# Putting the conditional slots without tokens in front of those that have tokens, in an attention and mixture-of-experts kernel

## The chip, the cores and the metric

The kernel runs on one core of a Trainium2 chip. The metric is the device time of one execution in microseconds (us). Timed executions of the kernel before took 885.78 us in the median of three (880.81 to 892.82). The profile is that of another, separate execution, which took 846.87 us and has a span of 845.1 us from its first instruction to its last, so a step read in the profile is a little shorter than in the timed runs. Engines are called PE (TensorE, matrix multiplication), PEld (its weight loads), DVE (VectorE), ACT (ScalarE), POOL (GpSimd) and SP (SyncE, which issues most transfers here). A "q" after a name (SPq, PEldq, POOLq) means the sequencer of that engine: branches, semaphores, register loads and the issuing of transfers.

## What is computed

Two blocks, one after the other. The first is windowed attention (8 batches, 8 heads, 576 positions, head size 64). Its output becomes a table of 4608 tokens of width 512. The second is a mixture of experts without dropped tokens: each token goes to the one expert with the highest logit, and that expert is a two-layer network.

```python
logits = x @ w_gate                       # x: 4608 x 512, 8 experts
expert_idx = np.argmax(logits, axis=1)
...                                       # gate_w: softmax probability of that expert
for e in range(E):
    h = np.maximum(x_sorted[lo:hi] @ w1[e], 0.0)    # 512 -> 1024
    y_sorted[lo:hi] = h @ w2[e]                     # 1024 -> 512
return gate_w[:, None] * y
```

How many tokens an expert gets is known only on the chip. The kernel therefore works in slots of 128 tokens of one expert. 4608 tokens make 36 full slots, and since each of the 8 experts may end with a partly filled slot, there can be up to 43. Slots 0 to 35 are always worked on. Slots 36 to 42 are conditional: each stands inside a runtime `If`, which lets it run only if it has tokens. With these inputs 39 slots have tokens, so 36, 37 and 38 run and 39 to 42 are skipped.

## The kernel before

Each slot needs three transfers: `x`, 128 rows of tokens (257 KB); `w1`, the first weight matrix of its expert (2 MB); `w2`, the second (2 MB). Two buffers hold `w1` and two hold `w2`; even slots use one of each, odd slots the other. If a slot has the same expert as the slot two before it, its weights are already there, and the transfer is issued with a condition that is false, so that it moves nothing. Three buffers hold `x`.

```python
NSLOT = (N + E * 127) // 128      # 43
SURE = N // 128                   # 36
...
"eidx": np.tile(np.minimum(np.arange(E1), E - 1), (128, 1)),   # "no expert" is read as expert 7
...
# new[j]: does slot j need other weights than slot j - 2?
nc.vector.tensor_tensor(out=new[:, lo - j0 : K], in0=exs[:, lo:j1],
                        in1=exs[:, lo - 2 : j1 - 2], op=OP.not_equal)
...
def fetch_x(j):                                                            # line 676
    x = xs[j] = mpool.tile([128, ROW], F32, tag="x", name=f"x_{j}", bufs=3)
    at0 = nc.sync.value_load(basei[:, n : n + 1], ...)                     # line 679
    read_bucket(nc.sync.dma_start(x, bucket[ds(at0, 128), :]), b)          # line 680

def fetch_w(j, dst, src):
    rv = nc.sync.value_load(exi[:, n : n + 1], ...)                        # line 684
    if j >= 2:
        kw["cond"] = nc.sync.value_load(newi[:, n : n + 1], ...) > 0       # line 687
    nc.sync.dma_start(dst[j % 2], src[ds(rv, 1)]..., **kw)                 # line 688

wanted = []
for j in range(NSLOT):
    wanted += [(j, "x", 0, j - 1), (j, "w1", 0, j - 1), (j, "w2", 1, j - 1)]
done = [0, 0]          # slots whose first / second layer has been written into the program

def fetch():           # issues, in the order of the list, all that may be issued by now
    while wanted and wanted[0][0] in where and done[wanted[0][2]] >= wanted[0][3]:
        ...

def across(j):         # turns x of slot j: 4 PE transposes and a DVE copy (lines 713, 715)
    ...

for j in range(NSLOT):
    if j >= SURE:
        while late:
            late.pop(0)()                          # the scatter of the slot before
        guards.close()
        guards.enter_context(tc.If(live[0] > j))   # line 725
    ...
    for fg in range(2):                            # first layer
        ...                                        # 32 matmuls into ph (line 739), twice
        if fg == 0:
            ...
            if j + 1 in xs:
                nxt = across(j + 1)
        else:
            done[0] = j + 1
            fetch()
    ...                                            # second layer: 16 matmuls into py (line 763)
    nc.scalar.activation(y, py, AF.Copy, scale=x[:, DM : DM + 1])          # line 767
    late.append(scatter)                           # indirect DMA on POOL (line 772)
    done[1] = j + 1
    fetch()
    xt = nxt
while late:
    late.pop(0)()
guards.close()                                     # line 790
```

So the transfers of a slot are issued while the slot before it is being worked on, and for conditional slots the issue stands inside the `If` of that slot before.

Of the kernel before, what the change touches and what calls it, by code (L numbers as in the profile page):

```python
# [10 lines left out]
F32 = mybir.dt.float32  # L11
I32 = mybir.dt.int32
AF = mybir.ActivationFunctionType
OP = mybir.AluOpType
# [6 lines left out]
N, DM, E, F = B * S, H * DH, 8, 1024  # L21
# [9 lines left out]
NSLOT = (N + E * 127) // 128  # L31
NROWS = E * CAP + 128
NOWHERE = 1.0e6
E1 = E + 1
SURE = N // 128


READY = [max(0, -(-(S * (b + 1) - E * 127) // 128)) for b in range(B)]
READY[B - 1] = NSLOT
# [5 lines left out]
def _constants():  # L45


    def band(j, ty):

        qi, ki = 64 * j + np.arange(64)[:, None], max(0, 64 * j - WIN) + np.arange(96)[None]  # L50
        seen = (qi - ki >= 0) & (qi - ki < WIN)
        if ty:
            seen &= qi // STRIP == ki // STRIP
        return np.where(seen, 0.0, BIG)

    def mask(ty):

        pairs = [(0, 1), (2, 3), (4, 5), (6, 7), (8, 8)]
        return np.concatenate([np.concatenate([band(j, ty) for j in two]) for two in pairs], 1)

    p = np.arange(128)
    e = np.arange(E)
    parts = {
        "mask0": mask(0),
        "mask1": mask(1),
        "tri": np.triu(np.ones((128, 128)), 1)[:, :96],
        "ones": np.ones((128, 128)),
        "rev": np.tile(E - e, (128, 1)),
        "ecap": np.tile(e * CAP, (128, 1)),
        "tok": p[:, None] + TT * np.arange(NT)[None],  # L70
        "row": p[:, None],
        "eidx": np.tile(np.minimum(np.arange(E1), E - 1), (128, 1)),
        "twice": np.tile(2 * np.arange(NSLOT), (128, 1)),
    }
    parts["first"] = np.tile(np.append(np.arange(E)[::-1] / E, -1e6), (128, 1))


    for s, (_, j0, j1) in enumerate(STAGES):
        k = np.arange(j1 - j0)
        n = (j1 - j0 + 1) // 2 if j1 < NSLOT else 0  # L80
        parts[f"list{s}"] = np.tile(k // 2 + n * (k % 2), (128, 1))
        parts[f"odd{s}"] = np.tile(k % 2, (128, 1))
    at, k, cols = {}, 0, []
    for name, a in parts.items():
        full = np.zeros((128, a.shape[1]), np.float32)
        full[: a.shape[0]] = a
        at[name] = (k, a.shape[1])
        k += a.shape[1]
        cols.append(full)
    return np.ascontiguousarray(np.concatenate(cols, 1)), at  # L90
# [3 lines left out]
def kernel(  # L94
# [10 lines left out]
    nc = tc.nc  # L105
# [3 lines left out]
    cpool = ctx.enter_context(tc.tile_pool(name="cpool", bufs=1))  # L109
# [18 lines left out]
    nc.vector.memset(used, 0.0)  # L128
    avail = cpool.tile([128, E1], F32, name="avail")
    nc.vector.memset(avail[:, E:E1], 4.0 * NSLOT)  # L130
    exs = cpool.tile([1, NSLOT], F32, name="exs")

    def const(name, rows=128):
        a, w = at[name]
# [393 lines left out]
    def tables(s):  # L528


        b, j0, j1 = STAGES[s]
        last, K = j1 == NSLOT, j1 - j0
# [8 lines left out]
        p = 128 if last else 1  # L541
# [8 lines left out]
        if last:  # L550
# [5 lines left out]
                out=far, in0=ns, scalar=128.0, in1=pad, op0=OP.mult, op1=OP.is_le  # L556
            )
            nc.vector.scalar_tensor_tensor(
                out=pad, in0=far, scalar=NOWHERE, in1=pad, op0=OP.mult, op1=OP.add
# [13 lines left out]
            out=upto,  # L573
            in0=key.unsqueeze(1).broadcast_to([1, E1, E1]),
            in1=key.unsqueeze(2).broadcast_to([1, E1, E1]),
            op=OP.is_ge,
# [4 lines left out]
            out=ends,  # L581
            in0=av.unsqueeze(1).broadcast_to([1, E1, E1]),
            in1=upto,
            op=OP.mult,
# [5 lines left out]
        if last:  # L590
# [7 lines left out]
                out=placed, in0=const(f"odd{s}", 1), scalar=half, in1=place,  # L598
                op0=OP.mult, op1=OP.add,
# [15 lines left out]
        def experts(a):  # L615
            return a.unsqueeze(1).broadcast_to(shape)

        sel, ge = table("sel", K, E1), table("ge", K, E1)
# [10 lines left out]
            out=first[:, 0:E], in0=us[:, 0:E], in1=begin[:, 0:E], op=OP.subtract  # L629
        )  # L630
        nc.vector.scalar_tensor_tensor(
            out=first[:, 0:E], in0=first[:, 0:E], scalar=128.0, in1=const("ecap", 1),
            op0=OP.mult, op1=OP.add,
# [5 lines left out]
            out=base, in0=place, scalar=128.0, in1=base, op0=OP.mult, op1=OP.add  # L639
# [12 lines left out]
        new = table("new", K)  # L652
        if j0 == 0:
            nc.vector.memset(new[:, 0:2], 1.0)
        lo = max(j0, 2)
        if lo < j1:
            nc.vector.tensor_tensor(
                out=new[:, lo - j0 : K], in0=exs[:, lo:j1], in1=exs[:, lo - 2 : j1 - 2],
                op=OP.not_equal,
            )  # L660
        yield
        ints = []
        for name, a in (("exi", ex), ("basei", base), ("newi", new)):
            i = mpool.tile([1, K], I32, tag=f"{name}{s}", name=name, bufs=1)
            nc.vector.tensor_copy(i, a)
            ints.append(i)
        for j in range(j0, j1):
            where[j] = (b, j - j0, *ints)
# [23 lines left out]


    wanted = []
    for j in range(NSLOT):
        wanted += [(j, "x", 0, j - 1), (j, "w1", 0, j - 1), (j, "w2", 1, j - 1)]
    done = [0, 0]

    def fetch():
        while wanted and wanted[0][0] in where and done[wanted[0][2]] >= wanted[0][3]:  # L700
            j, what, _, _ = wanted.pop(0)
            if what == "x":
                fetch_x(j)
            else:
                fetch_w(j, *((w1s, moe_w1) if what == "w1" else (w2s, moe_w2)))

    def moe():


        def across(j):  # L710
            ps = bank("xt", 4, 128)
            for c in range(4):
                nc.tensor.transpose(ps[:, c], xs[j][:, 128 * c : 128 * c + 128], ident)  # L713
            xt = mpool.tile([128, 4, 128], F32, tag="xt", name="xt")
            nc.vector.tensor_copy(xt, ps)  # L715
            return xt

        late = []
        xt = None
        for j in range(NSLOT):  # L720
            if j >= SURE:

                while late:
                    late.pop(0)()
                guards.close()
                guards.enter_context(tc.If(live[0] > j))
            x = xs[j]
            if xt is None:
                xt = across(j)
                yield 0.5  # L730
            h = mpool.tile([128, 8, 128], F32, tag="h", name="h")
            w1, w2 = w1s[j % 2], w2s[j % 2]
            nxt = None
            for fg in range(2):
                ph = bank("ph", 4, 128)
                for fi in range(4):
                    f = 4 * fg + fi
                    for c in range(4):
                        nc.tensor.matmul(  # L739
                            ph[:, fi],  # L740
                            lhsT=w1[:, c, 128 * f : 128 * f + 128],
                            rhs=xt[:, c],
                            start=c == 0,
                            stop=c == 3,
                        )
                    if fi < 3:
                        yield 0.93
                if fg == 0:
                    nc.scalar.activation(h[:, 0:4], ph, AF.Relu)  # L749
                    while late:  # L750
                        late.pop(0)()
                    yield 0.93
                    if j + 1 in xs:
                        nxt = across(j + 1)
                        yield 0.5
                else:
                    nc.vector.tensor_scalar(h[:, 4:8], ph, 0.0, None, op0=OP.max)  # L757
                    done[0] = j + 1
                    fetch()
                    yield 0.93  # L760
            py = bank("py")
            for f in range(8):
                nc.tensor.matmul(py, lhsT=h[:, f], rhs=w2[:, f], start=f == 0, stop=f == 7)  # L763
                if f < 7:
                    yield 0.88
            y = mpool.tile([128, DM], F32, tag="yo", name="y")
            nc.scalar.activation(y, py, AF.Copy, scale=x[:, DM : DM + 1])  # L767
            to = mpool.tile([128, 1], I32, tag="to", name="to", bufs=3)
            nc.vector.tensor_copy(to, x[:, DM + 1 : ROW])

            def scatter(y=y, to=to):
                i = nc.gpsimd.indirect_dma_start(  # L772
                    out=out,
                    out_offset=bass.IndirectOffsetOnAxis(ap=to, axis=0),
                    in_=y,
                    in_offset=None,
                    bounds_check=N - 1,
                    oob_is_err=False,
                ).ins
                tc.declare_no_dep(i, group="out", reason="no token is in two slots")  # L780
                tc.add_to_no_dep_group("out", i)

            late.append(scatter)
            done[1] = j + 1
            fetch()
            xt = nxt
            yield 0.88
        while late:
            late.pop(0)()
        guards.close()  # L790
# [88 lines left out]
```

## Time and profile before

| | |
|---|---|
| timed executions, median (lowest to highest) | 885.78 us (880.81 to 892.82) |
| profiled execution, span | 845.1 us |
| PE busy | 786.0 us, 93% |
| PEld busy | 591.5 us, 70% |
| DVE busy | 318.3 us, 38% |
| ACT busy | 203.6 us, 24% |
| POOL busy | 145.6 us, 17% |
| mean granted TensorE clock | 0.967 |
| moved by DMA | 187.42 MB |
| transfers of `w` issued (those with a false condition counted too) | 82 of 2048 KB |
| transfers of `x` issued | 41 of 257 KB |

A busy share is an average over the whole span. The kernel has a long first part in which attention and slots are interleaved, then a part with nothing but slots, and an end of some 19 us after the last matmul. What a change at the end of the program is worth is read in the last two of these alone.

### The profile page before, as it was taken

The numbers are of one execution on the slowest core, as the hardware profiler recorded it, in microseconds if no ns is written. First come the engines' busy times: TensorE is split into PE (matmuls) and PEld (weight loads), VectorE is DVE, ScalarE is ACT, GpSimd is POOL, SyncE is SP. The second block draws the span as 40 slices with busy tenths as digits, with TensorE's granted clock in tenths as the row PEclk, the third lists the DMA queues.
The fourth block names the chain that finished last, engine by engine and source line by source line (L and its number), as shares of the span: only waits on it lengthen the run. The fifth ranks groups of instructions, "written<-read, shape, count | busy, mean of one in ns | idle before, by whom it ended". The sixth has DMA issues, their size and how long they took to land.

```text
span 845.1 us, 17776 instructions
## 1 busy us (share of the span) xinstructions
PE 786.0 (93%) x6830; PEld 591.5 (70%) x6830; DVE 318.3 (38%) x955; ACT 203.6 (24%) x759; POOL 145.6 (17%) x139
## 2 busy tenths in 40 slices
PE   5778779999998999999999999999999999999991
PEld 4657668776676777777777777677776768686770
DVE  4788887647432543346333631411010101111110
ACT  2564463422222232232222221110000000010100
POOL 0214322213111221103111310240000000000000
PEclk8798799999999999999999999999999999999996
DMA  9968479898999869977455666799510661659574
GB/s 198 186 129 193 126 242 311 231 263 264 310 287 324 262 214 273 278 228 272 93 171 208 194 219 231 270 374 367 208 48 25 239 215 51 221 199 337 178 271 162
DMA packets 145721, 187.42 MB, mean 222 GB/s; under 512 B 72222, under 2 KB 86174, under 8 KB 145632
## 3 DMA queue, kind: packets, MB, share of 16 engines
q1 hardware_dynamic: 135316, 164.56, 64.1%
q0 software_dynamic: 6832, 19.71, 6.6%
q10 hardware_dynamic: 3484, 1.96, 1.1%
q8 instruction: 57, 0.93, 0.5%
q14 instruction: 32, 0.26, 0.1%
HBM read 216.56 MB, written 22.07 MB: 282 GB/s over the span
## 4 chain that ended last, share of the span: by engine, by line
PE 49%; issue 30%; DMA 6%; DVE 6%; POOL 3%; ACT 2%; SPq 1%; POOLq 0%; ACTq 0%; DVEq 0%
PE py L763 16%; PE ph L739 15%; PE xo L335 4%; DMA x<-bucket 4%; PE weights L320 3%; PE scores L272 3%; PE xrow L418 2%; POOL out_dram L772 2%; ACT e L295 2%; DMA k<-in_k_dram 2%; PE turned L237 2%; PE turned L245 1%; PE logits L428 1%; PE xt L713 1%; DVE lo L292 1%
## 5 line engine op out<-in xcount | busy, mean ns | idle before, releaser
L739 PE MATMUL ph<-xt,w 128*128 128x128 f32 x2496 | 304.8, 277 | 2.9 <-DVE xt L715 2.9
L739 PEld LDWEIGHTS ph<-xt,w 128*128 128x128 f32 x2496 | 292.2, 192 | 21.7 <-issue 16.9
L763 PE MATMUL py<-w,h 128*128 128x512 f32 x624 | 288.5, 600 | 0.5 <-DVE eT L322 0.5
L763 PEld LDWEIGHTS py<-w,h 128*128 128x128 f32 x624 | 110.8, 190 | 107.4 <-issue 104.3
L295 ACT ACTIVATE e<-e,lo 128x96 f32<-128x96 f32 x288 | 103.5, 362 | 68.4 <-DVE lo L292 64.6
L772 POOL DMA_INDIRECT out_dram<-y,to x39 | 38.7, 992 | 403.9 <-ACT y L767 369.0
L715 DVE COPY xt<-xt 128x512 f32<-128x512 f32 x40 | 27.5, 688 | 181.7 <-PE xt L713 181.6
L767 ACT ACTIVATE y<-py,x 128x512 f32<-128x512 f32 x39 | 26.8, 687 | 263.9 <-PE py L763 157.2
L310 POOL TENSOR_TENSOR e<-e,rec 128x864 f32<-128x864 f32 x32 | 52.2, 1631 | 201.9 <-DVE rec L309 117.0
L322 DVE COPY eT<-weights 96x384 f32<-96x384 f32 x96 | 48.3, 546 | 69.4 <-PE weights L320 68.9
L283 DVE SCALAR_TENSOR_TENSOR e<-scores,cst 128x384 f32<-128x384 f32 (+1 forms) x128 | 45.9, 398 | 44.4 <-PE scores L272 44.0
L757 DVE TENSOR_SCALAR h<-ph 128x512 f32<-128x512 f32 x39 | 26.9, 690 | 79.7 <-PE ph L739 79.6
L335 PEld LDWEIGHTS xo<-eT,v 96*64 96x64 f32 x1216 | 42.4, 144 | 18.5 <-issue 10.2
L295 ACT ACTIVATION_READ_ACCUMULATOR e<-e,lo 128x1 f32 x288 | 54.2, 188 | 0.0
L158 POOL DMA_INDIRECT bucket<-rows,idx x48 | 44.8, 933 | 37.0 <-DVE idx L517 22.8
L335 PE MATMUL xo<-eT,v 96*64 96x64 f32 (+1 forms) x1216 | 49.4, 232 | 0.0
L320 PE MATMUL weights<-ident,e 128*96 128x128 f32 x288 | 41.3, 293 | 7.0 <-POOL e L310 7.0
L749 ACT ACTIVATE h<-ph 128x512 f32<-128x512 f32 x39 | 23.2, 596 | 98.8 <-PE ph L739 98.8
L320 PEld LDWEIGHTS weights<-ident,e 128*96 128x96 f32 x288 | 34.0, 135 | 13.9 <-POOL e L310 7.9
L272 PEld LDWEIGHTS scores<-kT,qT 64*64 64x64 f32 x1152 | 31.6, 149 | 10.6 <-issue 6.6
L272 PE MATMUL scores<-kT,qT 64*64 64x96 f32 x1152 | 38.3, 271 | 0.1
L356 ACT COPY xT<-xo 128x288 f32<-128x288 f32 x32 | 21.1, 678 | 64.2 <-PE xo L335 64.2
(104 smaller groups left out, 461.4 us busy)
## 6 DMA issues: line engine op xcount, KB each, us to landing
w<-in_moe_w_dram SPq DMA_DIRECT2D x82, 2048.0 KB
x<-bucket SPq DMA_DIRECT2D x41, 257.0 KB
v<-in_v_dram SPq DMA_DIRECT2D x32, 192.0 KB
q<-in_q_dram SPq DMA_DIRECT2D x32, 144.0 KB
q<-in_q_dram SPq DMA_DIRECT2D x8, 576.0 KB
v<-in_v_dram SPq DMA_DIRECT2D x48, 96.0 KB
k<-in_k_dram SPq DMA_DIRECT2D x28, 144.0 KB
k<-in_k_dram SPq DMA_DIRECT2D x7, 576.0 KB
```

The lines of the kernel that those rows point to most:

```text
L158: nc.gpsimd.indirect_dma_start(out=bucket, out_offset=bass.IndirectOffsetOnAxis(ap=idx, axis=0), in_=rows, in_offset=None, bounds_check=NR ...
L272: nc.tensor.matmul(sc[r][64 * c : 64 * c + 64, 96 * (i % 5) : 96 * (i % 5) + 96], lhsT=qT[rows, 64 * j : 64 * j + 64], rhs=kT[rows, first_ ...
L283: nc.vector.scalar_tensor_tensor(out=e[p0:p1, i : i + n].rearrange("p i k -> p (i k)"), in0=sc[r][p0:p1, cols], scalar=-SCALE, in1=const(f ...
L295: nc.scalar.activation(out=e[:, n], in_=e[:, n], func=AF.Exp, bias=lo[:, n : n + 1], scale=-1.0, accum_out=den[:, n : n + 1],)
L310: nc.gpsimd.tensor_tensor(out=e, in0=e, in1=rec.unsqueeze(2).broadcast_to([128, 9, 96]), op=OP.mult)
L320: nc.tensor.transpose(tp[0:96, 128 * i : 128 * i + 128], e[:, a + i], ident)
L322: nc.vector.tensor_copy(eT, tp[0:96, 0:384])
L335: nc.tensor.matmul(xo[DH * h : DH * h + DH, at0 : at0 + nq], lhsT=vt[:, 2 * hl + r, j, :] if ty == 0 else vt[:, hl, j, DH * r : DH * r + D ...
L715: nc.vector.tensor_copy(xt, ps)
L739: nc.tensor.matmul(ph[:, fi], lhsT=w1[:, c, 128 * f : 128 * f + 128], rhs=xt[:, c], start=c == 0, stop=c == 3,)
L763: nc.tensor.matmul(py, lhsT=h[:, f], rhs=w2[:, f], start=f == 0, stop=f == 7)
L772: i = nc.gpsimd.indirect_dma_start(out=out, out_offset=bass.IndirectOffsetOnAxis(ap=to, axis=0), in_=y, in_offset=None, bounds_check=N - 1 ...
```

## The change

The slots are worked on in the order 0 to 35, then 42, 41, 40, 39, 38, 37, 36. Since the slots without tokens have the highest numbers, the skipped ones come directly after slot 35 and the ones with tokens come last. The purpose is that what the skipping of a slot costs no longer stands at the end of the program.

Four things go with it. Empty slots now have the expert number 99, which no slot with tokens has, and their `new` is set to zero, so that no weights are moved for them. The comparison for conditional slots looks at slot j + 2 instead of j - 2, as that one is now worked on two places earlier. The fetching for conditional slots moves out of the `If`, in front of it, because a skipped slot would otherwise not fetch for the one after it. And the turning of the next slot's `x` moves in front of the `If` too. The `x` of slots after place 36 is fetched one place earlier in relation to the work (place p - 2, counted by the second layer).

```diff
+WORK = [*range(SURE), *reversed(range(SURE, NSLOT))]
+NONE = 99
...
-        "eidx": np.tile(np.minimum(np.arange(E1), E - 1), (128, 1)),
+        "eidx": np.tile(np.where(np.arange(E1) < E, np.arange(E1), NONE), (128, 1)),
...
+        for lo, hi, step in ((max(j0, 2), min(j1, SURE), -2), (max(j0, SURE), j1, 2)):
+            if lo < hi:
+                nc.vector.tensor_tensor(
+                    out=new[:, lo - j0 : hi - j0], in0=exs[:, lo:hi],
+                    in1=exs[:, lo + step : hi + step], op=OP.not_equal,
+                )
         yield
+        if last:
+            nc.vector.scalar_tensor_tensor(
+                out=new, in0=sel[:, :, E], scalar=0.5, in1=new, op0=OP.is_lt, op1=OP.mult
+            )
...
-    for j in range(NSLOT):
-        wanted += [(j, "x", 0, j - 1), (j, "w1", 0, j - 1), (j, "w2", 1, j - 1)]
+    for p, j in enumerate(WORK):
+        x = (j, "x", 1, p - 2) if p > SURE else (j, "x", 0, p - 1)
+        wanted += [x, (j, "w1", 0, p - 1), (j, "w2", 1, p - 1)]
...
-        for j in range(NSLOT):
-            if j >= SURE:
+        for p, j in enumerate(WORK):
+            nxt = None
+            if p >= SURE:
                 while late:
                     late.pop(0)()
                 guards.close()
+                fetch()
+                if p + 1 < NSLOT:
+                    nxt = across(WORK[p + 1])
                 guards.enter_context(tc.If(live[0] > j))
...
-                    if j + 1 in xs:
-                        nxt = across(j + 1)
+                    if p < SURE and WORK[p + 1] in xs:
+                        nxt = across(WORK[p + 1])
...
-                    done[0] = j + 1
-                    fetch()
+                    done[0] = p + 1
+                    if p < SURE:
+                        fetch()
...
-            done[1] = j + 1
-            fetch()
+            done[1] = p + 1
+            if p < SURE:
+                fetch()
```

More of the change, by code (lines that the diff above doesn't have):

```diff
@@ L35 @@
 SURE = N // 128
+WORK = [*range(SURE), *reversed(range(SURE, NSLOT))]
+assert all(p % 2 == j % 2 for p, j in enumerate(WORK))
+NONE = 99
 READY = [max(0, -(-(S * (b + 1) - E * 127) // 128)) for b in range(B)]
@@ L130 @@
     nc.vector.memset(avail[:, E:E1], 4.0 * NSLOT)
-    exs = cpool.tile([1, NSLOT], F32, name="exs")
+    exs = cpool.tile([1, NSLOT + 2], F32, name="exs")
+    nc.vector.memset(exs[:, NSLOT : NSLOT + 2], float(NONE))
     def const(name, rows=128):
@@ L654, in tables @@
             nc.vector.memset(new[:, 0:2], 1.0)
[L655 to L659, printed above, removed]
+        for lo, hi, step in ((max(j0, 2), min(j1, SURE), -2), (max(j0, SURE), j1, 2)):
[4 more added lines that the diff above has]
+                )
+        yield
+        if last:
+            nc.vector.scalar_tensor_tensor(
+                out=new, in0=sel[:, :, E], scalar=0.5, in1=new, op0=OP.is_lt, op1=OP.mult
             )
-        yield
         ints = []
@@ L664, in tables @@
             i = mpool.tile([1, K], I32, tag=f"{name}{s}", name=name, bufs=1)
-            nc.vector.tensor_copy(i, a)
+            nc.vector.tensor_scalar(i, a, float(E - 1 if name == "exi" else NROWS), None, op0=OP.min)
             ints.append(i)
@@ L732, in moe @@
             w1, w2 = w1s[j % 2], w2s[j % 2]
-            nxt = None
             for fg in range(2):
```

## The prediction

> **What bounds the kernel now.** I began with the page, its slices.
>
> ```profile
> PE   5778779999998999999999999999999999999991
> ...
> PEclk8798799999999999999999999999999999999996
> DMA  9968479898999869977455666799510661659574
> ```
>
> From slice 8 on PE is busy 90% or more at full clock; only the last slice (21 us) is empty. So PE sets the time up to the last matmul, and the end is set by something else. The change touches only the places after slot 35, so I read those. The timeline of PE gives the pace of a slot:
>
> ```profile
> 768.46 3.73 PE L739 MATMUL ph<-xt,w 128*128 128x128 f32 x32
> ...
> 782.91 3.73 PE L739 MATMUL ph<-xt,w 128*128 128x128 f32 x32
> ...
> 797.36 2.84 PE L739 MATMUL ph<-xt,w 128*128 128x128 f32 x24
> ```
>
> One slot takes 14.45 us, and there is no gap where the `If`s begin (the first is in front of slot 36, at 782.91). Slots 36, 37 and 38 start at 782.91, 797.36 and 811.81; the last matmul ends at 826.42. From there to 845.1 are **18.7 us of tail**.
>
> The table of stretches shows which weights moved (last three columns: clock, DMA share, GB/s):
>
> ```profile
> 792.00:794.00 2.00, 2.00 (x6) 0.83 (x5) 0.00 (x0) 0.00 (x0) 0.00 (x0) 1.00 0.05 20
> ...
> 824.00:826.00 2.00, 2.00 (x6) 0.76 (x4) 0.00 (x0) 0.00 (x0) 0.00 (x0) 1.00 1.02 410
> ...
> 830.00:832.00 2.00, 0.00 (x0) 0.00 (x0) 0.00 (x0) 0.00 (x0) 0.00 (x0) 0.59 0.99 316
> 834.00:836.00 2.00, 0.00 (x0) 0.00 (x0) 0.00 (x0) 0.00 (x0) 0.00 (x0) 0.50 0.33 120
> ```
>
> DMA is still from 792 to 806: the `w1` issued at 790.68 and the `w2` issued at 797.55, slot 38's, moved nothing, so slot 38 has slot 36's expert. From 806 to 835 it runs almost without a break: those are `w1`, `w2` of slots 39 and 40, 8.4 MB that no slot uses. They hurt nothing before 826, and the last ends near 835. The answers by line for the end of an `If` and of the program show what lasts longer:
>
> ```profile
> L725 PEldq COMPARE_BRANCH  x9: 73/174/468, 777.7 to 827.3; - x9
> L725 POOLq INC_SWDGE_SEM  x3: 2035/2046/2080, 827.6 to 832.1; - x3
> ...
> L790 PEldq COMPARE_BRANCH  x1: 4662/4662/4662, 827.7 to 827.7; - x1
> L790 POOLq INC_SWDGE_SEM  x1: 2035/2035/2035, 834.3 to 834.3; - x1
> ...
> L875 POOLq DRAIN  x3: 51/107/7833, 836.4 to 844.8; - x3
> ```
>
> For each of the four skipped slots POOL raises the semaphore of a scatter that did not happen, 2.04 us each. It does so after the last scatter (827.47), from 827.58 to 836.38, and only then begins its 7.83 us DRAIN, which leads to the end. **The tail is POOL's**: 1.05 to the scatter, 8.9 of raising, 7.8 of DRAIN, 0.85 of final semaphores.
>
> **What the Trainium skill says.** (1) "DMA: Bandwidth & Descriptors", section "Queues, rings and completion order": one issuing engine has one ring on each DMA engine, and each ring is consumed in order. A small `x` behind two weight matrices therefore arrives after them. No single line here proves it, but the trace fits: the `x` issued on a quiet queue at 798.85 moved by 802; the one issued at 784.46, behind a `w2`, had the DMA busy until 792. (2) "TensorE: Matmul & The Clock Gate", "What's actually happening": after an idle window of about 3.4 us the clock halves, and it takes about such a window of work to return. The trace agrees: 0.59 in the stretch that starts 3.6 us after the last matmul, then 0.50. (3) "Runtime: NRT & Kernel Launch", "Instruction fetch mechanics": a taken branch out of the prefetched instructions stalls. PE's branches took 0.07 to 0.47 us, one 4.66.
>
> **The change part by part.** Call T the end of slot 35's matmuls (782.9 in this trace).
>
> *What it takes away.* The raising moves in front of slots 38, 37, 36, where POOL has over 20 us before its next scatter: hidden. DRAIN starts right after the last scatter, at 828.5 instead of 836.4. If it keeps its 7.8 us, the tail is 1.05 + 0.97 + 7.83 + 0.85 = 10.7, a gain of 8.0; if it gets shorter, the scatter's own landing (6.8 us on the page) still holds the end to some 9. I take **-8.5**. The 8.4 MB saved gain nothing themselves.
>
> *What it adds.* Before, slot 36's `w1` was issued while slot 35 ran. Now slot 38 is the first real slot after 35, at place 40, and its weights are issued only at place 39, after SP has gone through the fetches of places 37 to 39. SP works in order, and it cannot pass T: `w2` of place 37, though it moves nothing, waits for slot 35's last use of that buffer, and `x` of place 38 waits for slot 35's `y`. The pace of SP from its rows:
>
> ```profile
> L684 SPq TENSOR_LOAD <-exi x82: 263/272/697, 113.5 to 815.4; - x82
> ...
> L687 SPq TENSOR_LOAD <-newi x78: 260/266/631, 161.2 to 816.3; - x78
> ```
>
> and from the timeline of SP, at the first slots:
>
> ```profile
> 113.09 0.39 SPq L680 DMA_DIRECT2D x<-bucket  x1
> 114.28 1.60 SPq L688 DMA_DIRECT2D w<-in_moe_w_dram  x2
> 116.67 3.30 SPq L680 DMA_DIRECT2D x<-bucket  x1
> ```
>
> The burst at 113 has three issues in 3.58 us (113.09 to 116.67), without any `newi` load: 1.2 us each. A conditional weight adds that load: its 0.27, the 0.15 of the register operation after it, the check, and gaps, some 0.75; a false one saves 0.3 of issue. So 1.65 for a false weight, 1.2 to 1.36 for an `x` (1.36 from 783.10 to 784.46): **4.6 us for a place**. Then:
> - T + 1.4: `x` of place 38 is issued.
> - Two places later, T + 10.6: `x` of place 40, slot 38's own.
> - T + 12.4: `w1` of slot 38; about T + 14: its `w2`; about T + 15: `x` of place 41 (slot 37).
> - PE does `across` of slot 37 in front of the `If` of slot 38, in order. So slot 38 waits for an `x` that stands behind its own `w1` and `w2` in the ring. 4.19 + 0.26 MB at 390 GB/s (between the 373 and 410 of the stretches) are 11.4 us, plus some 1.4 from issue to first byte and to the semaphore: T + 25.2.
> - Four transposes and semaphores, 1: slot 38 starts at **T + 26**. Before, a slot started at T.
>
> If `w2`'s register loads are done ahead of `w1`'s issue, as SP did at 785 to 787, this is 1.5 later: I take **+27**. Afterwards nothing more waits: slot 37's weights and slot 36's `x` follow in the ring and are there by about T + 39, and slot 38 ends after T + 41. Slot 36 has slot 38's expert and moves nothing.
>
> *Clock.* 27 us of near idleness halve it. Slot 38 starts with 3.4 to 6.8 us at half speed: 1.7 to 3.4 lost, **+2.5**. *Small DVE additions* in the last table: one more operation, under 0.5 us, with DVE 38% busy; 0.
>
> Sum: +27 + 2.5 - 8.5 = **+21 us**; 885.8 + 21 = 906.8, and with a little for branches 907, a ratio of 1.024.
>
> **Rivals.**
> - *The weights are hidden anyway.* Then only the tail counts: 877. For it: four skipped slots ought to let SP run ahead. Against it: every fetch of places 37 to 39 stands behind T, and a false transfer takes the same waits.
> - *Slot 38 waits for `w1` only*, as `x` of slot 37 overtakes: 2.1 MB at 390 GB/s end at T + 19.2, some 20 for the start. +20 + 2.5 - 8.5 = +14: 900, within 2%. Against it: one ring in order.
> - *Fetching of instructions.* The four skips on PE come close together. Each can stall like the 4.66 us, and the false weights on SP wait until PE has passed its `If`. One such stall lies beside SP's own work; three would add some 5: 912.
> - *The skipping costs nothing on the path in either place*, since DRAIN stretches to the same end: no gain in the tail, 915.
>
> **Range and chances.** The bound of faster by 2% is 868, below even the first rival: 0.05. The bound of slower is 903.5, 3.5 below my number. SP's pace and the bandwidth may each be off by 3, the clock by 2, the tail by 2, the timed runs by 5: about 7 together. That gives slower 0.65, same 0.30. Range 894 to 919.
>
> **What would show it.** One gap on PE of 24 to 30 us after slot 35, with only transposes in it, which ends with an `x` and not with a `w`; `w1` of slot 38 issued at T + 12 to 14; half clock at slot 38's start; no gap between the last three slots; the four raisings beside the gap; a tail of 9 to 11 us; some 8 MB less moved. I am wrong if SP issues slot 38's weights before T, if PE's gap ends with `w1`, or if DRAIN lasts longer without the raisings.

## The result: 25 us slower, and the profile after

The changed kernel takes 910.65 us in the median of six executions (907.72 to 913.09), the kernel before 885.47 us beside it. The ratio is 1.0274, with a 95% interval of 1.0226 to 1.0322: **slower**, by some 25 us, as predicted (907, 21 us more).

A warning before traces are compared. The same kernel takes a different time from chip to chip: the kernel before took 848 to 849 us on two of the chips of this study and 884 to 890 us on two others. That it is the chip itself, and not the hour, is not shown. The profile shown in front was of the shorter kind, that of the changed kernel is of the longer. So slot 35 ends at 782.9 us in the one and at 824.1 us in the other, and those 41 us are not the change's, as e4 below shows. All that follows counts from T, the end of slot 35's matmuls, or uses ratios to the kernel before on the same chip.

First the slices of the page:

```profile
PE   4777788799999999999999899799999999993595
...
PEclk9988788899999999999999899989999999996698
DMA  9865559998898759974474466889412816333800
```

The end was one empty slice before. Now PE has a hole in the slices 37 and 38 (the 3 and the 5, 22.8 us each) with the clock at 6 tenths, then one full slice, and half of the last one is work. DMA is still in the last two. The timeline of PE shows the hole. Each line is start, duration, what ran, how often, and in brackets the idle time before it and what ended it:

```profile
817.22 7.03 PE L780 MATMUL py<-w,h 128*128 128x512 f32 x16
824.09 0.27 PE L725 MATMUL xt<-ident,x 128*128 128x128 f32 x1
...
828.11 0.45 PE L725 MATMUL xt<-ident,x 128*128 128x128 f32 x1 [3.08 <-DMA x<-bucket]
...
837.54 0.45 PE L725 MATMUL xt<-ident,x 128*128 128x128 f32 x1 [3.46 <-DMA x<-bucket]
...
852.43 0.45 PE L725 MATMUL xt<-ident,x 128*128 128x128 f32 x1 [13.35 <-DMA x<-bucket]
852.69 10.22 PE L755 MATMUL ph<-xt,w 128*128 128x128 f32 x64
...
870.93 7.38 PE L755 MATMUL ph<-xt,w 128*128 128x128 f32 x64 [0.72 <-ACT y L784]
...
886.34 7.38 PE L755 MATMUL ph<-xt,w 128*128 128x128 f32 x64 [0.83 <-PE xt L725]
893.56 7.03 PE L780 MATMUL py<-w,h 128*128 128x512 f32 x16
```

T is 824.09. Slot 38 starts at 852.69, **28.6 us later**; before, a slot started at T. The last and longest wait in the hole, 13.35 us, ends with an `x` (slot 37's) and not with a `w`. The first layer of slot 38 takes 10.22 us instead of 7.38: half clock for its first part. And slots 37 and 36 start 15.41 us apart instead of 14.45, each after a short wait that I had not foreseen.

SP's timeline shows why the `x` is late:

```profile
825.20 0.34 SPq L691 DMA_DIRECT2D x<-bucket  x1
827.08 1.93 SPq L699 DMA_DIRECT2D w<-in_moe_w_dram  x2
829.85 0.34 SPq L691 DMA_DIRECT2D x<-bucket  x1
831.73 1.93 SPq L699 DMA_DIRECT2D w<-in_moe_w_dram  x2
834.82 0.34 SPq L691 DMA_DIRECT2D x<-bucket  x1
836.73 2.54 SPq L699 DMA_DIRECT2D w<-in_moe_w_dram  x2
840.11 2.06 SPq L691 DMA_DIRECT2D x<-bucket  x1
843.70 2.62 SPq L699 DMA_DIRECT2D w<-in_moe_w_dram  x2
```

The three `x` up to 834.82 are those of places 38, 39 and 40, 4.65 and 4.97 us apart. Between them go pairs of weights that move nothing. The pair at 836.73 (T + 12.6) is slot 38's, and the `x` at 840.11 is the one PE waits for.

And the end, from the answers by line:

```profile
L739 POOLq INC_SWDGE_SEM  x4: 1975/1986/2002, 825.8 to 832.4; - x4
...
L893 POOLq DRAIN  x3: 45/113/8898, 901.6 to 911.0; - x3
```

POOL's four raisings now lie in the hole, and DRAIN begins with the last scatter, so that its 8.90 us contain the scatter's 0.97. Counted from the end of POOL's last instruction it ends after 7.85 us, as before (7.87): without the raisings it did not get longer. The last matmul ends at 900.59, so the tail is 10.7 us instead of 18.7. The page's total moved by DMA fell from 187.42 to 179.55 MB: four useless weights of 2.1 MB less, two `x` more.

| part, us | predicted | first profile of after | second (e4) |
|---|---|---|---|
| slot 38 starts after T by | 27 | 28.6 | 28.1 |
| half clock at slot 38 | 2.5 | 2.8 | 1.5 |
| two waits at slots 37 and 36 | 0 | 1.9 | 1.9 |
| one `x` fewer turned among the last three slots | 0 | -0.4 | -0.4 |
| tail | -8.5 | -8.0 | -8.0 |
| sum | +21 | +24.9 | +23.1 |
| measured, medians | | +25.2 | +22.1 |

### The profile page after: what moved, and what is told of

Same layout as the page of the kernel before. It is cut to its first block, busy times and chain, and to the rows that moved or that the text cites. A ratio compares the mean times of both kernels' runs of the same rounds, so it can differ in the third digit from the quotient of the medians.

```text
span 911.3 us, 17857 instructions
## 1 busy us (share of the span) xinstructions
PE 814.3 (89%) x6842; PEld 610.0 (67%) x6842; DVE 321.6 (35%) x961; ACT 203.6 (22%) x759; POOL 145.4 (16%) x139
## 2 busy tenths in 40 slices
DMA packets 142872, 179.55 MB, mean 197 GB/s; under 512 B 72190, under 2 KB 86142, under 8 KB 142784
## 5 line engine op out<-in xcount | busy, mean ns | idle before, releaser
L755 PE MATMUL ph<-xt,w 128*128 128x128 f32 x2496 | 313.6, 281 | 12.8 <-issue 8.6
L755 PEld LDWEIGHTS ph<-xt,w 128*128 128x128 f32 x2496 | 299.2, 196 | 31.5 <-issue 25.1
L727 DVE COPY xt<-xt 128x512 f32<-128x512 f32 x43 | 29.7, 690 | 200.2 <-PE xt L725 198.5
L325 PE MATMUL weights<-ident,e 128*96 128x128 f32 x288 | 45.4, 310 | 9.6 <-POOL e L315 7.0
L725 PE MATMUL xt<-ident,x 128*128 128x128 f32 x172 | 30.0, 294 | 26.4 <-DMA x<-bucket 22.9
L340 PE MATMUL xo<-eT,v 96*64 96x64 f32 (+1 forms) x1216 | 51.3, 238 | 0.0
L325 PEld LDWEIGHTS weights<-ident,e 128*96 128x96 f32 x288 | 37.0, 144 | 17.2 <-POOL e L315 8.0
L277 PE MATMUL scores<-kT,qT 64*64 64x96 f32 x1152 | 40.9, 274 | 5.8 <-issue 5.5
```

The lines of the kernel that those rows point to most:

```text
L277: nc.tensor.matmul(sc[r][64 * c : 64 * c + 64, 96 * (i % 5) : 96 * (i % 5) + 96], lhsT=qT[rows, 64 * j : 64 * j + 64], rhs=kT[rows, first_ ...
L325: nc.tensor.transpose(tp[0:96, 128 * i : 128 * i + 128], e[:, a + i], ident)
L340: nc.tensor.matmul(xo[DH * h : DH * h + DH, at0 : at0 + nq], lhsT=vt[:, 2 * hl + r, j, :] if ty == 0 else vt[:, hl, j, DH * r : DH * r + D ...
L755: nc.tensor.matmul(ph[:, fi], lhsT=w1[:, c, 128 * f : 128 * f + 128], rhs=xt[:, c], start=c == 0, stop=c == 3,)
```

## The experiments

**Controls: e0, the kernel before once more, and e4, the kernel after once more.** No edit.

> The kernel before, unchanged, for a second profile. Its first profile (845.1 us) is some 39 us shorter than its timed runs (885.5 us), and slot 35 ended there at 782.9 us, but at 824.1 us in the kernel after. If the change left everything up to slot 35 alone, this run takes some 885 us, slot 35 ends near 824 us, and the tail after the last matmul is again 18.7 us. If the change itself lengthened the part before slot 35, slot 35 ends near 783 us here.

> The kernel after, unchanged, on a chip beside the kernel before. In the second profile of the kernel before, slot 35 ended at 794 us and not at 824 us as in the profile of after, while the same part is 784 to 789 us in the three variants of after. Theory: the part up to slot 35 varies with the chip and the execution, whatever the kernel, so here after costs its 24 to 26 us over the kernel before of the same chip, of which none lies ahead of slot 35: gap 28.6, slower clock 2.8, two small gaps 1.9, tail 7.8 less. Rival: the change also slows the part before slot 35; then the end of slot 35 lies some 30 us behind that of the kernel before here too, and the total is more than 40 us over it.

e0 took 858.1 us on a chip where the kernel before has a median of 848.1; slot 35 ended at 794 us. My first theory for it, 885 us and an end near 824, was wrong: I had not thought of the chip. The tail was again 18.7 us. e4 settles it. On its chip the kernel before takes 884.6 us and after 906.7, a ratio of 1.025 (1.018 to 1.032). Slot 35 ended at 817.5 us in e4, and at 824.9, 817.5 and 817.2 in the three kernels with the old order that ran beside it (e5 to e7). So nothing can be seen of the change ahead of T.

**e1, the `x` in front of the weights; e2, no weight transfers for the empty slots; e3, both.** Each is the kernel after with the list of transfers changed. e2 leaves out transfers that move nothing here; other inputs would need them.

```diff
 # e1
-        wanted += [x, (j, "w1", 0, p - 1), (j, "w2", 1, p - 1)]
+        ws = [(j, "w1", 0, p - 1), (j, "w2", 1, p - 1)]
+        if p > SURE + 2:
+            wanted[-2:-2] = [x]
+            wanted += ws
+        else:
+            wanted += [x, *ws]
 # e2
+        wanted += [x]
+        if p not in range(SURE, SURE + 4):
+            wanted += [(j, "w1", 0, p - 1), (j, "w2", 1, p - 1)]
```

> The kernel after, with only the order in the list of transfers changed: from place 39 on, the x of a slot is issued in front of the weights of the slot before it instead of behind them. Theory: slot 38 waited for the x of slot 37, which stood behind 4.2 MB of weights in the ring; now it waits for its own w1 alone, which is issued one x later (T + 13.9 instead of T + 12.6) and lands some 7 us after that. Slot 38 starts near T + 21 instead of T + 28.6, and the time falls by 7.5 us to about 903. Rival, that the gap is only SP's pace through the fetches of the skipped slots: it grows by the 1.2 us of one more x, 912.

> The kernel after, with the weight transfers of slots 42 to 39 left out (with these inputs they move nothing; a general kernel would need them). Theory: SP's pace through them, some 3.3 us for a pair, holds back slot 38's w1, so that w1 is issued near T + 7 instead of T + 12.6 (no sooner, because the buffer is free only when PE has passed the If of slot 40, which it reaches after the x of slot 39 has landed). The x of slot 37 still stands behind the weights. The gap shrinks by 5 to 6 us and the time falls to about 905. Rival, that the ring alone makes the gap and SP's pace is hidden: no change, 910.

> Both edits: no weight transfers for slots 42 to 39, and the x of the next slot in front of the weights. Theory: the two shares of the gap are separate and add: w1 of slot 38 issued near T + 8, slot 38 starts near T + 15.5, 13 us less than after, about 897. If one of them only hid the other, the sum is not more than the larger of the two single gains (about 903).

The timelines of PE, e1 first:

```profile
811.14 9.65 PE L760 MATMUL ph<-xt,w 128*128 128x128 f32 x64 [6.41 <-DMA w<-in_moe_w_dram]
```

then e2:

```profile
809.23 0.45 PE L727 MATMUL xt<-ident,x 128*128 128x128 f32 x1 [11.89 <-DMA x<-bucket]
809.48 10.19 PE L757 MATMUL ph<-xt,w 128*128 128x128 f32 x64
```

and e3:

```profile
800.27 8.95 PE L762 MATMUL ph<-xt,w 128*128 128x128 f32 x64 [4.38 <-DMA w<-in_moe_w_dram]
```

| | T | `w1` of slot 38 issued | slot 38 starts | its wait ends with | ratio to before (interval) |
|---|---|---|---|---|---|
| after (e4 for the ratio) | 824.09 | T + 12.6 | T + 28.6 | `x` | 1.025 (1.018 to 1.032) |
| e1 | 788.40 | T + 14.5 | T + 22.7 | `w1` | 1.0215 (1.0145 to 1.0286) |
| e2 | 787.57 | T + 6.4 | T + 21.9 | `x` | 1.0246 (1.0184 to 1.0309) |
| e3 | 784.07 | T + 6.8 | T + 16.2 | `w1` | 1.0137 (1.0082 to 1.0192) |

The order alone takes 5.9 us off the hole, the missing pairs alone 6.7, both 12.4: the two shares add. With the `x` in front, PE's wait ends with `w1`, as it must if the `x` had been held behind 4.2 MB. It had been a real wait in a queue, and so had SP's walk. The rivals (the hole is SP's pace alone, or the ring's alone) are out. The ratios of e1 and e2 overlap with that of after, so the proof lies in the starts, not in the totals; that of e3 just overlaps with e4's and lies clear of the first measurement's (1.0226 to 1.0322). The 16.2 us that are left in e3 are 6.8 until `w1` is issued and 9.4 until the first layer, which waits for it, starts; no run of the changed order took these away.

**e5, what the tail was; e9, whether the useless weights cost anything.** e5 is the kernel before with `range(39)` in place of `range(NSLOT)` in its two loops over the slots; it leaves out the empty slots, which other inputs need. e9 is the kernel before with the changed table alone (`eidx` with 99, `new` set to zero for slots without tokens).

> The kernel before without slots 39 to 42: their Ifs, and the 8.4 MB of weights fetched for 39 and 40, are left out of the program, so it would be wrong for other inputs. Theory: the tail was POOL's raising of four semaphores, 8.9 us; it falls from 18.7 to some 10.9 us, and the time by 8 us. Rival: DRAIN stretches to the same end, or the landing of the last scatter holds the end: less than 2 us.

> The kernel before with only the changed table: slots without tokens have expert 99 and ask for no weights, so that the 8.4 MB for slots 39 and 40 are not moved. Order and everything else as before. Theory: these transfers ended 8.6 us after the last matmul, before POOL had done its raising, and nothing waited for them; no change, ratio 1.000 within 0.003. Rival: they held back the last scatter or the end; 2 to 3 us less.

By line at the program's end, e5:

```profile
L875 POOLq DRAIN  x3: 45/112/8898, 868.8 to 878.2; - x3
```

and e9:

```profile
L879 POOLq DRAIN  x3: 51/107/7833, 840.1 to 848.5; - x3
```

with, in e9's table of stretches, a still DMA where the kernel before moved 300 to 400 GB/s:

```profile
832.00:836.00 4.00, 0.00 (x0) 0.00 (x0) 0.00 (x0) 0.00 (x0) 0.13 (x1) 0.88 0.13 45
836.00:840.00 4.00, 0.00 (x0) 0.00 (x0) 0.00 (x0) 0.00 (x0) 0.00 (x0) 0.50 0.00 0
```

Without the raisings (and the useless weights), e5's tail is 10.7 us, and the time falls by 7.3 us: ratio 0.9896 (0.9868 to 0.9924). Without the useless weights but with the raisings, e9's tail is 18.7 as before, ratio 0.9985 (0.996 to 1.001). The tail was POOL's, and the 8.4 MB were hidden under it.

**e6, the idea without its cost.** The kernel of e5 with four skipped `If`s in front of slot 36:

```diff
+                if j == SURE:
+                    for n in range(NSLOT - 1, 38, -1):
+                        with tc.If(live[0] > n):
+                            i = nc.gpsimd.indirect_dma_start(out=out, ...)   # writes no row
```

> The kernel before without slots 39 to 42, and with four Ifs put in front of slot 36 that hold only a scatter which writes no row; all four are skipped, so that POOL raises its four semaphores there. Nothing is fetched or turned for them, and slots 36 to 38 keep their order and their early transfers. It is the idea of the change without its cost. Theory: the raising hides beside slot 36, and the time is that of the kernel without slots 39 to 42, 8 us under the kernel before; PE loses at most 1 us at the four Ifs. Rival: skipping itself costs time wherever it stands; then it is no faster than the kernel before.

Ratio 0.9861 (0.979 to 0.993), tail 10.7 us, no gap on PE. The raisings did not stand where I had put them, by line:

```profile
L730 POOLq INC_SWDGE_SEM  x4: 1635/1638/1662, 583.2 to 588.8; - x4
```

Nothing tied these `If`s to slot 35, so the compiler moved them to 583 us, among the attention work. So e6 is not quite the kernel I meant, but it still says that four skipped scatters cost nothing that can be seen where POOL has time for them and nothing has to be fetched for the slots (e10 below has them beside slot 36). What makes the change slow is the fetching behind T.

**e7, e8, e10, e11: a version that beats both.** e7 and e8 leave the order of slots alone and move the scatters of slots 36 to 42 out of their `If`s; each of these slots gets a `y` and a `to` of its own. In e7 the scatters are unconditional. In e8 each stands in an `If` after all other work:

```diff
+        for j in (42, 41, 40, 39, 36, 37, 38):
+            with tc.If(live[0] > j):
+                late[j - SURE]()
```

> The kernel before, order unchanged, with the scatters of slots 36 to 42 moved out of the Ifs: each conditional slot has a y and a to of its own, to is preset so that a skipped slot's scatter writes no row. It is general. POOL then does four scatters of 0.97 us in place of four raisings of 2.2 us at the end. Theory: the tail falls by 4 to 5 us, to 14 us, and the time by 4.5 us, the ratio to the kernel before 0.995. Rival: DRAIN after five scatters takes longer and eats it: same or slower than before.

> The kernel before with all its work in the old order, except that the scatters of slots 36 to 42 stand after it in the program, each in an If of its own, in the order 42, 41, 40, 39, 36, 37, 38, and that each of these slots has a y and a to of its own. It is general; the order only suits inputs with at most three conditional slots. POOL, which has nothing else to do, passes the four skipped scatters while slot 36 is still being worked on. Theory: the tail falls from 18.7 to 10.9 us as in the kernel without slots 39 to 42, no other engine sees a difference, and the time falls by 7 to 8 us: ratio 0.991, faster than both kernels. Rival: POOL's branches or the raising wait for the work of the skipped slots on the other engines, which is passed only after slot 38; then the tail stays near 18.7 us.

e7's timeline of POOL:

```profile
861.59 0.97 POOL L783 DMA_INDIRECT out_dram<-yc,toc  x1 [12.98 <-ACTq L727]
862.86 0.97 POOL L783 DMA_INDIRECT out_dram<-yc,toc  x1 [0.30 <-issue]
864.14 0.97 POOL L783 DMA_INDIRECT out_dram<-yc,toc  x1 [0.30 <-issue]
...
866.69 0.97 POOL L783 DMA_INDIRECT out_dram<-yc,toc  x1 [0.30 <-issue]
```

A scatter takes 0.97 us, but the next starts 1.28 later. The tail is 16.2 us, 2.5 less than before instead of 4 to 5; ratio 0.9978 (0.9956 to 1.0000), so that a gain is hardly clear of none. e8 was a miss, 1.0084 (1.0051 to 1.0117). By line:

```profile
L801 POOLq INC_SWDGE_SEM  x4: 2035/2040/2080, 834.2 to 841.4; - x4
```

The last matmul ended at 832.4: the raisings stood at the end again, in a tail of 19.8 us. My reading, not shown, is that the compiler sorts the scatters by when their data is ready, and that the empty slots come last in that. So e8 says nothing on the theory, only that the order in the source is not the order on the engine. Of its 5.6 us only 1.1 lie in the tail; where the other 4.5 arose was not looked for. e10 ties the order down, by making the scatters of 36 to 38 depend on the earlier ones:

```diff
-            def scatter(y=y, to=to):
+            def scatter(y=y, to=to, free=not SURE <= j < SURE + 3):
-                tc.declare_no_dep(i, group="out", ...)
+                if free:
+                    tc.declare_no_dep(i, group="out", ...)
```

> As e8, where the compiler had put the three scatters with tokens in front of the four skipped ones, because nothing tied them to each other, so that POOL raised its four semaphores at the end as before. Here the scatters of slots 36, 37 and 38 are declared to follow those of 39 to 42 (the freedom to reorder writes of the output is taken back for these three), and POOL's program has 39, 40, 41, 42, 36, 37, 38. Theory: as for e8, POOL raises the four beside slot 36, the tail is 10.9 us instead of 18.7, and the time falls by 7 to 8 us, ratio 0.991. What could spoil it: each of the three scatters now waits until the one before has landed, some 7 us, which is less than a slot's 14.45; and the last branches of e8, which cost 1 us more in the tail than the kernel before. Rival: the waits for skipped slots on other engines hold POOL until slot 38 is done; then the tail is 18 us or more.

By line in e10:

```profile
L802 POOLq INC_SWDGE_SEM  x4: 1975/1986/2002, 823.1 to 830.1; - x4
...
L888 POOLq DRAIN  x3: 45/113/11237, 865.5 to 877.3; - x3
```

The raisings lie beside slot 36 (820.5 to 835.0), and the ratio is 0.9939 (0.992 to 0.9959): faster than both kernels, though by 0.6% only. But the tail is 13.6 us and not 10.9, because DRAIN took 11.24. e11 adds the table of e9.

> The kernel of e10 with the table of e9 added, so that the 8.4 MB of weights for slots 39 and 40 are not moved either. In e10 POOL's DRAIN ended 10.2 us after its last scatter; in the kernels where no weights are in flight at the end (after, e5, e6) it ended 7.85 us after it. Theory: DRAIN waits for the last scatter to land, and in e10 that shares the DMA engines with the useless w2, now that POOL's raising no longer covers it; without it DRAIN ends 7.85 us after the scatter, the tail falls from 13.6 to some 11.3 us, and the ratio to the kernel before from 0.994 to 0.991. Rival: DRAIN is longer in e10 for another reason, such as the three scatters' waits or the many branches; no change against e10.

```profile
L892 POOLq DRAIN  x3: 45/112/8892, 866.0 to 875.5; - x3
```

DRAIN is back at 8.89 and the tail at 11.2 us; ratio 0.9886 (0.9843 to 0.9928). The useless weights, which cost nothing under POOL's raising (e9), lengthen DRAIN once the raising is gone. That they do so through the landing of the last scatter, as I wrote, is not shown. The last of the scatter's 16 completion signals came 6.3 us after the scatter in e10 (872.83) and 2.1 after it in e11 (869.10), so the weights do hold it back. But that is 4.2 us more, while DRAIN lasted only 2.35 longer: it is not the landing plus a fixed time. e11 leaves nothing out that other inputs need, and has the lowest ratio of the kernels of which that is true; its order suits at most three conditional slots with tokens. The intervals of e10 and e11 still overlap a little, so that e11 is the faster of the two rests on the tails, from one profile each.

## Why the prediction was right, step by step

- **The bound and the tail.** Right. I took 8.5 us, of which 8.0 was worked out and 0.5 was a hope that DRAIN would shorten. It kept its length: the tail is 10.7. (Two readings were loose, and nothing rests on them: slice 13 of PE has an 8, and between 800 and 802 an `x` moved where I called DMA still.)
- **SP's walk behind T.** Right. 4.6 us for a place against 4.65 and 4.97; `w1` at T + 12.4 against T + 12.6. e2 shows that it is a cost and not only a delay beside another.
- **The `x` behind the weights.** Right in kind, which e1 shows, and low in size. From the issue of `w1` to the `x` I had 12.8 us, measured 15.6 (836.73 to 852.33, where PE's sequencer passes that wait). The rate was as assumed, as the stretches show:

```profile
836.00:840.00 4.00, 1.32 (x4) 0.69 (x4) 0.75 (x2) 0.00 (x0) 0.00 (x0) 0.50 0.64 185
840.00:844.00 4.00, 0.00 (x0) 0.00 (x0) 0.00 (x0) 0.00 (x0) 0.00 (x0) 0.50 1.02 410
844.00:848.00 4.00, 0.00 (x0) 0.00 (x0) 0.00 (x0) 0.00 (x0) 0.00 (x0) 0.50 1.03 393
848.00:852.00 4.00, 0.00 (x0) 0.00 (x0) 0.00 (x0) 0.00 (x0) 0.00 (x0) 0.50 1.04 401
```

  But from 836 to 852.3 some 5.7 MB moved (185, 410, 393 and 401 GB/s for 4 us each and 0.3 us more), while two weights and the two last `x` are 4.7. The trace also holds 16 completion signals for each transfer, and they show what happened meanwhile. Of those of this `x`, 15 came between 849.99 and 850.76 and the last at 852.30; the two weights ahead of it also had one late signal each (844.70 and then 846.21; 850.07 and then 851.63). So one sixteenth of the transfer was 1.5 us behind, and PE waited for it, while the remaining 1 MB can only be slot 37's weights, issued from 843.7 on, which the other fifteen had begun. That is 1.5 of the 2.8 us; the other 1.3 are not separated. The sentence of the Trainium skill on which I built ("DMA: Bandwidth & Descriptors", "Queues, rings and completion order") speaks of each ring, and I had reckoned as if there were one. My 1.5 us for register loads done ahead did not happen, which by luck made up for half of it.
- **The clock.** Right: 2.8 and 1.5 us against 2.5. The two profiles of the same kernel differ by 1.3 us here, which fits what "TensorE: Matmul & The Clock Gate" says under "What's actually happening", that the window runs free.
- **"No gap between the last three slots".** Wrong, by 0.96 us at slots 37 and 36. In the source the four transposes of the next `x` stand in front of the `If`, but in after's trace only the first ran there (852.43, PE's branch at 852.45). The other three ran behind the slot's second layer, at 869.61 and at 885.02, and DVE's copy of the turned `x` came after them:

```profile
885.02 0.49 PE L725 MATMUL xt<-ident,x 128*128 128x128 f32 x3
...
885.55 0.69 DVE L727 COPY xt<-xt 128x512 f32<-128x512 f32 x1 [6.45 <-PE xt L725]
...
886.34 7.38 PE L755 MATMUL ph<-xt,w 128*128 128x128 f32 x64 [0.83 <-PE xt L725]
```

  So a slot waits for its own `x` to be turned. (For slot 37 the profile names the `y`, but DVE's copy ended later, at 870.83, and the slot starts at 870.93.) In e1 all four ran in front of the slot before (at 803.64 for slot 37, at 827.49 for slot 36), and no wait is left.
- **The rivals.** Hidden weights, waiting for `w1` only, and no gain in the tail are each refuted by the profile after. PE's branches at the skipped `If`s took up to 0.42 us each, and no long stall was among them.

## What to carry to other kernels

Work that is skipped at run time still holds its place in every in-order queue: its transfers, its buffers and its semaphores. In this kernel moving it out of the tail paid only where what follows it could be fetched without passing through it (e10, e11); in the change the place in front of real work was dearer than the end (28.6 us against 8.0). And an order that matters must be tied by a dependency: the compiler moved what was free in e6, in e8 and, with three of four transposes, in the change itself.

## What the hardware showed unexpectedly

- The kernel before takes 848 us on some chips and 885 us on others. Of the part up to slot 35, where the difference lies, no single cause was looked for; PE was busy 89% and 100% in the stretch from 500 to 600 us in the profiles of after and before.
- POOL's long DRAIN ended 7.8 to 7.9 us after POOL's last instruction, be it a scatter or a raising, in before, after, e5, e6, e9 and e11, 8.2 us after it in e7, and 10.2 us after it in e10, where 2 MB of weights were in flight.
- One of the 16 completion signals of a transfer on SP's queue came 1.5 us after the other fifteen, three times in a row (846.21, 851.63 and 852.30 in after), and PE's wait for the `x` ended only with that one.
- SP's issue of a transfer took 0.34 us, but 6.5 us for the `x` at 847.17 in after, with two pairs of weights queued ahead: the issue itself can block.
